# An attention stage and two mixtures of experts on one core: an overflow-only table, a gathered weight table, token counts and the order of loads and fillers are rearranged

## The chip, the cores and the metric

The kernel runs on one core of one Trainium2 chip. The metric is the device time of one execution in microseconds (us). The kernel before was timed three times: 796.45 us is the median, 795.43 the lowest and 799.09 the highest. The trace is of a separate profiled execution.

The names of the engines: PE is the matrix engine, PEld its weight loads, DVE the vector engine, ACT the scalar engine, POOL the GpSimd engine, and SP the engine that here only issues DMA transfers.

## The reference

```python
# 1. attention with decay: x (4,8,768,32), a (4,8,768), B and C (4,8,768,16), in chunks of 32
la = log_a[:, :, sl]; cum = np.cumsum(la, axis=-1)
M = np.einsum('bhin,bhjn->bhij', Cc, Bc) * exp(cum_i - cum_j) * causal
y[:, :, sl] = M @ xc + (Cc @ state) * exp(cum)[..., None]
state = exp(sum(la)) * state + sum_j Bc_j xc_j exp(cum_last - cum_j)
x = y.transpose(0, 2, 1, 3).reshape(3072, 256)
# 2. first mixture: 8 experts (256 -> 1024 -> 256), each token goes to one
probs = softmax(x @ w_gate); expert_idx = argmax(x @ w_gate)
for e in range(8):
    out[mask] = gate_w[mask, None] * (np.maximum(x[mask] @ w1[e], 0) @ w2[e])
# 3. second mixture: 4 experts of the same sizes, each sees all 3072 tokens
p = domain_probs / (domain_probs.sum(-1, keepdims=True) + 1e-9)
out = sum(p[:, e:e + 1] * (np.maximum(x @ w1[e], 0) @ w2[e]) for e in range(4))
```

All arrays are fp32.

## The kernel before

**Attention, to about 102 us.** The 3072 tokens are 24 tiles (`NU`) of 128. A loop `i = 0..24` is written as a software pipeline: in iteration `i` the scores of tile `i+1`, the matmuls `y` of tile `i` (`within`, `across`, L507), and the transposing matmuls and the store of tile `i-1` (`stage_c`, `store`) are issued. There is no scheduler here: each engine runs its instructions in the order in which the program writes them, so an instruction that waits holds back everything behind it on its engine. `load` fetches two tiles of `xb`; `load_bc` fetches a block `cz` (128 x 3 x 384 floats, 576 KB) into one of three buffers, and `bc_head` scales it on ACT to `cm`. `store` copies the router's logits `lg` and the tile `xo` out of PSUM on ACT and sends `xo` to the array `xs` in DRAM. On SP eight DMA semaphores are used in turn, so that a transfer is issued only when the one eight places before it has landed.

**The opening** loads `au`, clips it to `ah`, and makes decay factors by the matmuls `abc` (`decay`, L469) and `pfp` (`decays_c`, L451). `warm(n)` puts `n` matmuls of a unit matrix in front of them, whose result nothing uses.

**Expert 0's weights** come in the loop as well. `WEIGHTS` and `SPLITS` say in which iteration a half of `w1` or `w2` begins to be loaded, and in which its split into a high and a low part begins. A half comes in four pieces, one per iteration (L142); the split takes four steps of two functions each, the high part a cast on ACT (L159), the low part a subtraction on POOL. The pieces of `w1` are column blocks and each cast needs the piece that it reads. The pieces of `w2` are row groups, while each cast takes a column block of all four: the first cast needs all pieces.

```python
WEIGHTS = {1: (0, 0), 5: (0, 1), 9: (1, 0), 13: (1, 1)}
SPLITS = {5: (0, 0), 9: (0, 1), 13: (1, 0), 17: (1, 1)}
...
    for f in ws[:2]:
        f()
    ws = ws[2:]
```

**Routing** follows in three groups of tiles, as they are finished (`GROUPS`). `route` gives a list of small functions (one-hot of the largest logit, `ranks` of the tokens within an expert by matmuls into `rk`, places, and `invert`, which turns the places into lists of tokens by one-hot products `om` and matmuls `ip`). They stand in `queue` and are taken by `slot()` at set points of an iteration; a `None` ends what one call takes. `early()` uses the count of expert 0 after the second group, and `ct` (L1016 to L1020) counts the tokens of all experts when all are routed.

**First mixture, about 102 to 268 us.** For each expert `gemm1x` (L273) makes the hidden values, with products of high and low parts, ACT the relu `hh`, DVE the remainder `hl` (L893), and `gemm2x` the output. Hooks after each step call `prep`, which splits the next expert's weights, and empty the lists `rest` and `queue`. In the queue stand also `places`, `weights2`, the last `invert` with `placed`, and 24 `fetch`es, that gather the weights of the second mixture by token from the DRAM table `pgd`. The list of places in DRAM, `idd`, has its tail filled with zeros in the attention loop (L741) and its body written by `placed` (L1062). Only the block `If left > 0` behind the first mixture reads it, for tokens that found no place; this execution does not take it.

**Second mixture, to the end.** The first weights of it, the pairs of blocks `v`, are loaded by `load_pair` (L177) and prepared by `sums_pair` (L187), whose sums overwrite part of the loaded tile, and `split_pair` (L193 to L197), in the hooks of expert 7. In the mixtures the order on an engine is settled when the kernel is built and is not everywhere the written one.

Of the kernel before, what the change touches and what calls it, by code (L numbers as in the profile page):

```python
# [43 lines left out]
def body(tc, I, out):  # L44
    nc = tc.nc
    with ExitStack() as outer:
# [25 lines left out]
        idc = cp.tile([P, NU], I32, name="idc")  # L72
        pgs = cp.tile([P, NU, E2], F32, name="pgs")
# [127 lines left out]
        def prep(g, step):  # L201
            if g == E1:
                if step < 2 and (g, step) not in RAW:
                    load_pair(g, step)
# [5 lines left out]
            elif g < E1:  # L210
                k = (g, step // 2, step % 2)
                if k not in RAW:
                    load_w(*k)
                fs = split_w(*k, 1 + k[1])
                m = 2 if k[1] else len(fs)
                for f in fs[:m]:
                    f()
                rest.extend(fs[m:])

        def invert(rt, place, g0, n, ncol, finish, psum, bufs=2, off=0, eng=nc.vector):  # L220
# [25 lines left out]
            def mm():  # L246
                ip = o["ip"] = psum([P, ncol], name="ip")
                for i in range(n):
# [5 lines left out]
                    + hots + [None, None, mm, None] + [lambda: finish(o["ip"])])  # L254
# [57 lines left out]
        with ExitStack() as ctx:  # L312
# [32 lines left out]
            bc_part, bc_head = load_bc(0)  # L345
            bc_part(0, P, nc.scalar)
# [3 lines left out]
            nc.scalar.copy(d0, zero.bitcast(F32))  # L350

# [225 lines left out]
            def route(g0, n, psum, between=()):  # L577
# [24 lines left out]
                def ranks():  # L602
                    rk = o["rk"] = psum([P, n, E1], name="rk")
                    nc.tensor.matmul(rk, tri_b, oh, start=True, stop=False)
                    for i in range(n - 1):
                        nc.tensor.matmul(rk[:, i + 1:, :], ones_b,
                                         oh[:, i:i + 1, :].broadcast_to([P, n - 1 - i, E1]), start=False, stop=False)
                    nc.tensor.matmul(rk, ones_b, before[:, None, :].broadcast_to([P, n, E1]),
                                     start=False, stop=True)

                def finish(ip):
# [15 lines left out]
                    lambda: (v.tensor_mul(rs, o["rk"], oh), between and between[0]()),  # L627
                    lambda: v.tensor_reduce(r1, rs, axis=AX.X, op=ALU.add),
                    lambda: v.scalar_tensor_tensor(sl, r1, float(TRASH), m2, op0=ALU.min, op1=ALU.subtract),
                ] + list(between[1:]) + invert(rt, sl, g0, n, NC, finish, psum, off=OFF, eng=g if not g0 else v)  # L630
# [19 lines left out]
            def early():  # L650

                o = {}

                def count():
                    o["c"] = psum_a([P, E1], name="c0")
                    nc.tensor.matmul(o["c"], ones_b, before, start=True, stop=True)

                def shift():
                    v = nc.vector
                    c = o["c"][:, 0:1]  # L660
# [7 lines left out]
                return ([count, shift],  # L668
# [27 lines left out]
            warm(9)  # L696
            chunks[1]()
            decay(0)
            warm(2)
# [21 lines left out]
            WEIGHTS = {1: (0, 0), 5: (0, 1), 9: (1, 0), 13: (1, 1)}  # L721
            SPLITS = {5: (0, 0), 9: (0, 1), 13: (1, 0), 17: (1, 1)}
            DECAYS = {max(3 * m - 2, 2): m for m in range(1, NU // 3)}
            CHUNKS = {0: 3, 1: 4, 2: 2, 3: 5}
            for i in range(NU + 1):
# [14 lines left out]
                if i == 8:  # L740
                    nc.sync.dma_start(idd[NT:], zero)  # L741
                    queue += probs
# [179 lines left out]
        with ExitStack() as ctx:  # L922
# [93 lines left out]
            ct = pp.tile([P, E1], F32, tag="oneA", name="ct")  # L1016
            nc.tensor.matmul(ct, ones_b, before, start=True, stop=False)
            for u in range(ENDS[1] + 1, NU):
                nc.tensor.matmul(ct, ones_b, oneh[:, u], start=False, stop=(u == NU - 1))
            nc.scalar.copy(cnt, ct)  # L1020
# [38 lines left out]

            def placed(ip):  # L1060
                v.tensor_scalar(idc, ip, float(NT // 2), None, op0=ALU.add)
                nc.sync.dma_start(idd[:NT].rearrange("(u p) o -> p (u o)", p=P), idc)  # L1062

            def weights2():
                nc.gpsimd.tensor_mul(prob, prob, gate[:, :, None].broadcast_to([P, NU, E2]))
                nc.sync.dma_start(pgd.rearrange("(u p) e -> p u e", p=P), prob)

            def fetch(u):
                with tc.issue_after(LOW[0]) if LOW else ExitStack():
                    nc.gpsimd.indirect_dma_start(  # L1070
                        pgs[:, u, :], None, pgd, bass.IndirectOffsetOnAxis(ap=idc[:, u:u + 1], axis=0))
# [43 lines left out]
            with tc.If(left > 0), tc.tile_pool(name="fall", bufs=1) as fp:  # L1115
# [3 lines left out]

                st, n, ni, pc, lt = t8("st", (E1,)), t8("n", (E1,)), t8("ni", (E1,), I32), t8("pc", (E1,)), t8("lt", (E1, E1))  # L1120
# [286 lines left out]
```

## Time and profile before

| what | value |
|---|---|
| median of three timed runs | 796.45 us |
| the profiled execution's own time | 799.93 us |
| its span (first to last instruction) | 798.1 us |
| mean granted clock of PE, as a share of full speed | 0.98 |
| PE busy | 763.2 us, 96% |
| DVE, POOL, ACT busy | 573.2, 490.9, 414.1 us |
| DMA, mean over the span | 58 GB/s |

The span is what the trace shows; 1.8 us of the execution's time lie around it. Busy times of different engines overlap. A granted clock of 1.0 is 2.4 GHz, of 0.5 is 1.2 GHz; a value between them over a window is a mixture of the two.

### The profile page before, as it was taken

The page shows a single profiled execution, that of the slowest core. Times are in us where ns is not written, and L with a number is a line of the kernel's source. Part 1 is how long each engine was busy: PE and PEld are TensorE (multiplying, and loading weights), DVE is VectorE, ACT ScalarE, POOL GpSimd, SP SyncE. Part 2 cuts the span into 40 slices and gives each one's busy share as a digit, 9 for nine tenths or more (in the row PEclk, how much of TensorE's full clock was granted, in tenths as well). Part 3 has the DMA queues.
Part 4 walks back from the last instruction along what each step waited for, and adds up shares of the span by engine and source line. Part 5 has one row for each costly group of instructions (what it writes and reads, how often), then busy time and mean ns, then how long its engine had stood idle before and what let it go on. Part 6 is the DMA issues. An engine that isn't in the chain of part 4 may idle for free.

```text
span 798.1 us, 16869 instructions
## 1 busy us (share of the span) xinstructions
PE 763.2 (96%) x6508; PEld 714.8 (90%) x6508; DVE 573.2 (72%) x980; ACT 414.1 (52%) x939; POOL 490.9 (62%) x581
## 2 busy tenths in 40 slices
PE   8979889999998999999999999999999999999994
PEld 5555589899998899999999999999999999999894
DVE  5757955764464787869787678896776987878753
ACT  4656435444554554565655545656456565544540
POOL 4555657557864473658875458776366886575534
PEclk7999999999999999999999999999999999999998
DMA  6686236448531210001110000000001000000001
GB/s 179 178 152 191 76 107 210 96 163 100 163 107 54 55 54 1 1 11 44 28 27 2 1 2 27 27 27 28 1 1 28 28 1 1 1 35 21 27 27 53
DMA packets 41522, 46.57 MB, mean 58 GB/s; under 512 B 10592, under 2 KB 31072, under 8 KB 41440
## 3 DMA queue, kind: packets, MB, share of 16 engines
q1 hardware_dynamic: 36624, 37.09, 17.7%
q0 software_dynamic: 3360, 7.13, 2.9%
q10 hardware_dynamic: 1456, 1.25, 0.5%
q8 instruction: 52, 0.85, 0.5%
q14 instruction: 30, 0.25, 0.1%
HBM read 39.10 MB, written 6.35 MB: 57 GB/s over the span
## 4 chain that ended last, share of the span: by engine, by line
PE 59%; ACT 3%; DVE 2%; issue 1%; POOL 0%; POOLq 0%; ACTq 0%; DVEq 0%
PE po L1292 32%; PE x L1226 9%; PE z L1226 8%; PE w L1226 7%; PE y L1226 3%; ACT xc L852 1%; ACT s L1239 1%; DVE xc L853 1%; ACT h L1232 1%; DVE c L1266 0%; DVE c L1254 0%; POOL out L1312 0%; ACT s L1241 0%; DVE h L1235 0%; PE poA L1292 0%
## 5 line engine op out<-in xcount | busy, mean ns | idle before, releaser
L1292 PE MATMUL po<-w,h 128*128 128x256 f32 x2280 | 280.2, 281 | 0.3 <-DVE h L1235 0.3
L1292 PEld LDWEIGHTS po<-w,h 128*128 128x128 f32 x2280 | 277.6, 188 | 0.5 <-DVE h L1235 0.5
L1232 ACT ACTIVATE h<-c 128x384 fp32r<-128x384 f32 x192 | 98.6, 525 | 160.8 <-DVE c L1266 92.1
L1235 DVE SCALAR_TENSOR_TENSOR h<-c,h 128x384 fp32r<-128x384 f32 x192 | 153.3, 807 | 18.1 <-ACT h L1232 6.9
L1245 POOL TENSOR_TENSOR g<-s,s 128x384 f32<-128x384 f32 x64 | 65.0, 1016 | 110.4 <-ACT s L1243 110.4
L165 POOL TENSOR_TENSOR wl<-raw,wh 128x256 fp32r<-128x256 f32 x72 | 54.5, 783 | 54.1 <-ACT wh L159 52.9
L853 POOL TENSOR_TENSOR xc<-ts,xc 128x384 fp32r<-128x384 f32 x61 | 71.1, 1174 | 25.2 <-PE x L1226 14.0
L1247 DVE TENSOR_TENSOR u<-y,s 128x384 f32<-128x384 f32 x64 | 35.4, 553 | 57.4 <-ACT s L1243 57.1
L1226 PE MATMUL x<-xc,wh 128*128 128x384 f32 x256 | 68.4, 348 | 5.0 <-ACT s L1239 4.0
L1226 PE MATMUL w<-xc,wh 128*128 128x384 f32 x256 | 65.7, 337 | 0.5 <-DVE xc L853 0.5
L1226 PE MATMUL z<-xc,wh 128*128 128x384 f32 x256 | 65.5, 337 | 0.0
L1266 DVE TENSOR_TENSOR c<-u,g 128x384 f32<-128x384 f32 x63 | 64.5, 1024 | 0.0
L853 POOL TENSOR_TENSOR xc<-x,xc 128x384 fp32r<-128x384 f32 x31 | 36.4, 1173 | 42.7 <-ACT xc L852 42.7
L891 ACT ACTIVATE hh<-ph 128x216 fp32r<-128x216 f32 (+8 forms) x68 | 32.9, 491 | 49.1 <-PE ph L273 41.0
L273 PE MATMUL ph<-xh,wh 128*128 128x480 f32 (+8 forms) x142 | 49.6, 349 | 4.4 <-DVE hl L893 3.6
L1239 ACT COPY s<-x 128x384 f32<-128x384 f32 x64 | 30.5, 476 | 44.2 <-PE x L1226 44.2
L1235 DVE SCALAR_TENSOR_TENSOR h<-x,h 128x384 fp32r<-128x384 f32 x64 | 35.6, 557 | 24.2 <-ACT h L1232 23.5
L1226 PEld LDWEIGHTS x<-xc,wh 128*128 128x128 f32 x256 | 41.4, 188 | 12.2 <-ACT s L1239 10.2
L893 DVE SCALAR_TENSOR_TENSOR hl<-ph,hh 128x216 fp32r<-128x216 f32 (+8 forms) x68 | 36.7, 551 | 18.4 <-ACT hh L891 18.3
L273 PE MATMUL ph<-xl,wh 128*128 128x480 f32 (+8 forms) x142 | 48.4, 341 | 0.0
L273 PE MATMUL ph<-xh,wl 128*128 128x480 f32 (+8 forms) x142 | 48.2, 339 | 0.0
L912 PE MATMUL po<-hh,wh 128*128 128x480 f32 (+8 forms) x142 | 48.1, 339 | 0.0
(243 smaller groups left out, 1690.9 us busy)
## 6 DMA issues: line engine op xcount, KB each, us to landing
raw<-in_w SPq DMA_DIRECT2D x26, 512.0 KB, 4.1
raw<-in_v SPq DMA_DIRECT2D x32, 256.0 KB, 2.7
xb<-in_xb SPq DMA_DIRECT2D x22, 192.0 KB, 4.4
cz<-in_cb SPq DMA_DIRECT2D x7, 576.0 KB, 7.0
xs<-xo SPq DMA_DIRECT2D x24, 128.0 KB, 3.3
raw<-in_w SPq DMA_DIRECT2D x16, 128.0 KB, 5.1
raw<-in_w ACTq DMA_DIRECT2D x2, 512.0 KB
xg<-xs,idr POOLq DMA_INDIRECT x26, 3.9
```

Source lines behind the costliest of these rows:

```text
L165: ins = nc.gpsimd.tensor_sub(lo[:, :, a:a + n], raw[:, :, a:a + n], hi[:, :, a:a + n].bitcast(F32))
L273: mm = nc.tensor.matmul(ph, w[:, k, fs], x[k], start=(i == 0), stop=(i == 5))
L853: eng.tensor_sub(o[:, 1], src, o[:, 0].bitcast(F32))
L893: i1 = nc.vector.scalar_tensor_tensor(hl, ph, 0.0, hh.bitcast(F32), op0=ALU.max, op1=ALU.subtract)
L912: mm = nc.tensor.matmul(po, w[:, f % 4, ks], h, start=(i == 0), stop=(i == 23))
L1226: nc.tensor.matmul(bank[to], w[:, a], x[:, r], start=(m == 0 and to not in seen), stop=(m == 2), skip_group_check=True)
L1232: sc.activation(HP[n][0], src, AF.Relu)
L1235: v.scalar_tensor_tensor(HP[n][1], src, 0.0, HP[n][0].bitcast(F32), op0=ALU.max, op1=ALU.subtract)
L1239: sc.copy(s1, bank["x"])
L1245: nc.gpsimd.tensor_add(g_, s5, s7)
L1266: v.tensor_add(c22, u2, g_)
L1292: nc.tensor.matmul(two[h], x[:, ts], w2[:, w, j], start=(i, j, h * (len(hs) - 1), m) == (0, 0, 0, 0), stop=(i, j, m) == (3, 1, 2), skip_gr ...
```

## The change

1. The list of places `idd` is no longer written in the loop (L741) and in `placed` (L1062), but inside the block `If left > 0`.
2. The table of weights by token, `pgd`, is written with a partition's 24 rows together (`(p u) e`) instead of a tile's 128 rows together. The index of the gather is then not the token's number but its place in that table; `placed` computes it into `idg` with four more small operations on DVE.
3. The count of tokens per expert becomes one more slot of `rk`: `ranks` starts with the ones-matmul on `before`, adds the one-hots, and ends with the triangular one. `count` in `early` and the six matmuls `ct` with their copy go; `cnt` is copied from `rk`. `invert` has one more `None` ahead of the matmuls `ip`.
4. The first two pairs of blocks of the second mixture are loaded right behind the splits of expert 7's `w2` (through `rest`), and no longer at the head of `prep(E1, step)`.
5. In the opening ACT issues its load of the first third of `cz` behind the copy `d0` instead of ahead of it; `warm` has 10 and 4 matmuls instead of 9 and 2.
6. `WEIGHTS` starts one iteration earlier, `SPLITS` two.

```diff
         def prep(g, step):
             if g == E1:
-                if step < 2 and (g, step) not in RAW:
-                    load_pair(g, step)
                 if step < 3:
...
                 rest.extend(fs[m:])
+                if g == E1 - 1 and k[1]:
+                    rest.append(lambda: load_pair(E1, k[2]))
...
-                    + hots + [None, None, mm, None] + [lambda: finish(o["ip"])])
+                    + hots + [None, None, None, mm, None] + [lambda: finish(o["ip"])])
...
-            bc_part, bc_head = load_bc(0)
-            bc_part(0, P, nc.scalar)
             d0 = ac.tile([P, 1], F32, name="d0")
             ah = ac.tile([P, H, L], F32R, name="ah")
             nc.gpsimd.memset(ah[:, :, 0:1].bitcast(F32), 0.0)
             nc.scalar.copy(d0, zero.bitcast(F32))
+            bc_part, bc_head = load_bc(0)
+            bc_part(0, P, nc.scalar)
...
-                    rk = o["rk"] = psum([P, n, E1], name="rk")
-                    nc.tensor.matmul(rk, tri_b, oh, start=True, stop=False)
-                    for i in range(n - 1):
+                    rk = o["rk"] = psum([P, n + 1, E1], name="rk")
+                    nc.tensor.matmul(rk, ones_b, before[:, None, :].broadcast_to([P, n + 1, E1]),
+                                     start=True, stop=False)
+                    for i in range(n):
                         nc.tensor.matmul(rk[:, i + 1:, :], ones_b,
-                                         oh[:, i:i + 1, :].broadcast_to([P, n - 1 - i, E1]), start=False, stop=False)
-                    nc.tensor.matmul(rk, ones_b, before[:, None, :].broadcast_to([P, n, E1]),
-                                     start=False, stop=True)
+                                         oh[:, i:i + 1, :].broadcast_to([P, n - i, E1]), start=False, stop=False)
+                    nc.tensor.matmul(rk[:, :n], tri_b, oh, start=False, stop=True)
...
-                    lambda: (v.tensor_mul(rs, o["rk"], oh), between and between[0]()),
+                    lambda: (v.tensor_mul(rs, o["rk"][:, :n], oh), last and nc.scalar.copy(cnt, o["rk"][:, n])),
...
-            warm(9)
+            warm(10)
             chunks[1]()
             decay(0)
-            warm(2)
+            warm(4)
             decays_c(0)
...
-            WEIGHTS = {1: (0, 0), 5: (0, 1), 9: (1, 0), 13: (1, 1)}
-            SPLITS = {5: (0, 0), 9: (0, 1), 13: (1, 0), 17: (1, 1)}
+            WEIGHTS = {0: (0, 0), 4: (0, 1), 8: (1, 0), 12: (1, 1)}
+            SPLITS = {3: (0, 0), 7: (0, 1), 11: (1, 0), 15: (1, 1)}
...
                 if i == 8:
-                    nc.sync.dma_start(idd[NT:], zero)
                     queue += probs
...
-            ct = pp.tile([P, E1], F32, tag="oneA", name="ct")
-            nc.tensor.matmul(ct, ones_b, before, start=True, stop=False)
-            for u in range(ENDS[1] + 1, NU):
-                nc.tensor.matmul(ct, ones_b, oneh[:, u], start=False, stop=(u == NU - 1))
-            nc.scalar.copy(cnt, ct)
...
             def placed(ip):
                 v.tensor_scalar(idc, ip, float(NT // 2), None, op0=ALU.add)
-                nc.sync.dma_start(idd[:NT].rearrange("(u p) o -> p (u o)", p=P), idc)
+                v.tensor_scalar(t24, ip, float(NT // 2), float(NU), op0=ALU.add, op1=ALU.mult)
+                v.tensor_scalar(tile0, ip, float(NT // 2) - 63.5, float(BIG), op0=ALU.add, op1=ALU.add)
+                v.tensor_scalar(tile0, tile0, -float(BIG), 1.0 / P - NU, op0=ALU.add, op1=ALU.mult)
+                v.tensor_add(idg, t24, tile0)
...
-                nc.sync.dma_start(pgd.rearrange("(u p) e -> p u e", p=P), prob)
+                nc.sync.dma_start(pgd.rearrange("(p u) e -> p u e", p=P), prob)
...
+                nc.sync.dma_start(idd[:NT].rearrange("(u p) o -> p (u o)", p=P), idc)
+                nc.sync.dma_start(idd[NT:], zero)
```

**SP, iterations 8 to 12 of the attention loop, before** (`raw0` is a piece of `w1`, `raw1_0_0` and `raw1_0_1` are pieces of the two halves of `w2`, `xs` is the store of a tile):

```order
L741 DMA idd_68<-zero_70 128x1
L575 DMA xs_66<-xo_870 256x1x128
L142 DMA raw1_0_0_913<-in_w2 128x256
L575 DMA xs_66<-xo_938 256x1x128
L436 DMA xb1_147<-in_xb 64x2x384 x2
L142 DMA raw1_0_0_913<-in_w2 128x256
L575 DMA xs_66<-xo_1012 256x1x128
L337 DMA cz0_130<-in_cb 128x1152
L142 DMA raw1_0_0_913<-in_w2 128x256
L575 DMA xs_66<-xo_1078 256x1x128
L436 DMA xb2_148<-in_xb 64x2x384 x2
L142 DMA raw1_0_0_913<-in_w2 128x256
```

and in the changed kernel, from the same place:

```order
L143 DMA raw1_0_0_852<-in_w2 128x256
L576 DMA xs_66<-xo_881 256x1x128
L143 DMA raw1_0_0_852<-in_w2 128x256
L576 DMA xs_66<-xo_946 256x1x128
L437 DMA xb1_148<-in_xb 64x2x384 x2
L143 DMA raw1_0_0_852<-in_w2 128x256
L576 DMA xs_66<-xo_1020 256x1x128
L338 DMA cz0_131<-in_cb 128x1152
L143 DMA raw1_0_0_852<-in_w2 128x256
L576 DMA xs_66<-xo_1088 256x1x128
L437 DMA xb2_149<-in_xb 64x2x384 x2
L143 DMA raw1_0_1_1133<-in_w2 128x256
```

The write of `idd` is gone, and each piece of `w2` stands one iteration earlier; directly behind `cz0` stands now the fourth piece of `raw1_0_0` and not the third.

**ACT, before, around the first cast of `w2`** (on SP the fourth piece stands ahead of the store of `xo_1147`; `xo_1216` is the next tile's; `wh1` is the high part):

```order
L454 COPY pfg1_150<-pfp_1209 128x96x2
L455 COPY pf_1211<-pfp_1209 128x384
L573 COPY lg_99<-tp_1202 128x8
L574 COPY xo_1216<-tp_1202 128x264
L525 COPY yT_1245<-y_1220 128x2x2x64
L159 CAST wh1_0_0_1188<-raw1_0_0_913 128x4x64
```

and in the changed kernel, where `xo_1088` is what the store behind the fourth piece sends:

```order
L574 COPY lg_100<-tp_1078 128x8
L575 COPY xo_1088<-tp_1078 128x264
L526 COPY yT_1117<-y_1092 128x2x2x64
L341 ACTIVATE cm_850<-cz2_133,hmask_160 128x384 x2
L160 CAST wh1_0_0_1064<-raw1_0_0_852 128x4x64
L532 COPY U_1145<-S_1135 128x32
```

The first cast of `w2` stood in the iteration after that in which its last piece is issued, and stands now in the same iteration; `U`, the state's copy, which the next tile needs, stands right behind it on ACT.

**DVE, before, the begin of expert 7** (`raw0_8_0` and `raw0_8_2` are the tiles of `v` of the first and the third pair, on which `sums_pair` makes four sums each, `wl1_7` the low part of expert 7's `w2`, `hl` its hidden remainder):

```order
L307 TENSOR_TENSOR xl_3816<-tpx_3817,xh_3815 128x2x256
L307 TENSOR_TENSOR xl_3816<-tpx_3824,xh_3815 128x2x128
L187 TENSOR_TENSOR raw0_8_2_3967<-raw0_8_2_3967 128x128
L163 TENSOR_TENSOR wl1_7_0_3858<-raw1_7_0_3855,wh1_7_0_3857 128x4x128
L187 TENSOR_TENSOR raw0_8_2_3967<-raw0_8_2_3967 128x128 x3
L917 ISA
L917 COPY x21_2077<-po_3861 128x380
L163 TENSOR_TENSOR wl1_7_1_3890<-raw1_7_1_3887,wh1_7_1_3889 128x4x128
L893 SCALAR_TENSOR_TENSOR hl_3894<-ph_3909,hh_3893 128x368
```

and in the changed kernel:

```order
L308 TENSOR_TENSOR xl_3818<-tpx_3826,xh_3817 128x2x128
L164 TENSOR_TENSOR wl1_7_0_3860<-raw1_7_0_3857,wh1_7_0_3859 128x4x128
L911 ISA
L911 COPY x21_2082<-po_3863 128x380
L164 TENSOR_TENSOR wl1_7_1_3892<-raw1_7_1_3889,wh1_7_1_3891 128x4x128
L887 SCALAR_TENSOR_TENSOR hl_3896<-ph_3911,hh_3895 128x368
L164 TENSOR_TENSOR wl1_7_0_3860<-raw1_7_0_3857,wh1_7_0_3859 128x4x128
L164 TENSOR_TENSOR wl1_7_1_3892<-raw1_7_1_3889,wh1_7_1_3891 128x4x128
L887 SCALAR_TENSOR_TENSOR hl_3898<-ph_3933,hh_3897 128x368
L887 SCALAR_TENSOR_TENSOR hl_3900<-ph_3943,hh_3899 128x368
L887 SCALAR_TENSOR_TENSOR hl_3902<-ph_3953,hh_3901 128x368
L188 TENSOR_TENSOR raw0_8_0_3922<-raw0_8_0_3922 128x128 x3
```

The third pair's sums stood ahead of the splits and of all of expert 7's remainders. In the changed kernel the first sums on this engine are those of the first pair, behind four of the remainders; the third pair's stand behind the first two's.

## Rows read from the trace of the kernel before

**Rows 1.** The page's first part: busy time, share and instructions of each engine.

```profile
PE 763.2 (96%) x6508; PEld 714.8 (90%) x6508; DVE 573.2 (72%) x980; ACT 414.1 (52%) x939; POOL 490.9 (62%) x581
```

**Rows 2.** Windows: start:end, length, busy us (instructions) PE PEld DVE ACT POOL, clock, DMA share, GB/s.

```profile
8.50:22.00 13.50, 13.32 (x167) 6.78 (x169) 7.65 (x11) 5.65 (x19) 6.86 (x19) 0.50 0.55 155
50.00:55.00 5.00, 2.96 (x81) 1.79 (x68) 0.80 (x1) 1.88 (x7) 2.85 (x6) 1.00 0.99 59
55.00:60.00 5.00, 2.99 (x68) 1.97 (x68) 2.42 (x4) 1.86 (x7) 0.00 (x0) 0.63 0.70 149
60.00:65.00 5.00, 5.00 (x82) 2.94 (x74) 2.96 (x4) 3.12 (x11) 1.78 (x3) 0.69 0.88 279
185.00:190.00 5.00, 5.00 (x27) 4.83 (x27) 1.64 (x3) 1.08 (x3) 4.07 (x5) 1.00 0.95 34
250.00:255.00 5.00, 2.06 (x9) 1.76 (x10) 5.00 (x13) 0.95 (x2) 0.24 (x1) 0.93 0.14 30
255.00:260.00 5.00, 5.00 (x24) 5.00 (x23) 3.06 (x9) 2.67 (x5) 0.00 (x0) 0.73 0.27 93
```

**Rows 3.** Timeline, opening: start us, us, engine line operation out<-in, [idle before <-releaser].

```profile
5.19 0.29 DVE L417 TENSOR_SCALAR ah<-au 128x252 fp32r<-128x252 f32 x1 [1.06 <-DMA au<-in_au]
...
6.41 0.47 PE L469 MATMUL abc<-ah,pk 128*128 128x512 f32 x1 [0.96 <-ACT cm L340]
6.71 0.61 PE L426 MATMUL warm<-ident 128*128 128x128 f32 x4
8.19 1.32 PE L451 MATMUL pfp<-spare,sel 32*128 32x384 f32 x2 [0.87 <-DVE spare L397]
```

**Rows 4.** Timeline of PE, line 507 alone: some of the tiles' matmuls `y`.

```profile
15.48 0.68 PE L507 MATMUL y<-M,xb 64*32 64x64 f32 x32
20.20 0.68 PE L507 MATMUL y<-M,xb 64*32 64x64 f32 x32
25.71 0.46 PE L507 MATMUL y<-M,xb 64*32 64x64 f32 x32
28.53 0.45 PE L507 MATMUL y<-M,xb 64*32 64x64 f32 x32
...
52.66 0.30 PE L507 MATMUL y<-M,xb 64*32 64x64 f32 x4
57.01 0.76 PE L507 MATMUL y<-M,xb 64*32 64x64 f32 x28 [4.05 <-issue]
62.04 0.68 PE L507 MATMUL y<-M,xb 64*32 64x64 f32 x32
```

**Rows 5.** Timeline of SP around the write of `idd`: the write, and the ninth transfer from it.

```profile
45.43 0.42 SPq L741 DMA_DIRECT2D idd<-zero  x1
...
55.92 2.15 SPq L337 DMA_DIRECT2D cz<-in_cb  x1
```

**Rows 6.** Tile `idd`, the second write (L1062, at 179.1): from issue to landing.

```profile
DMA to landing us min/median/max: 15.1/15.1/15.1
```

**Rows 7.** Tile `raw` on SP, the piece issued at 34.8 (behind a `cz`).

```profile
L142 SPq DMA_DIRECT2D raw<-in_w x1: 443/443/443, 34.8 to 34.8; - x1
...
DMA to landing us min/median/max: 6.8/6.8/6.8
```

**Rows 8.** The same view, the piece issued at 27.9.

```profile
DMA to landing us min/median/max: 2.5/2.5/2.5
```

**Rows 9.** The page's sixth part, all pieces: count, KB each, median us to landing.

```profile
raw<-in_w SPq DMA_DIRECT2D x16, 128.0 KB, 5.1
```

**Rows 10.** Timeline of ACT, the cast in the iteration of the piece of rows 7.

```profile
36.93 0.39 ACT L159 CAST wh<-raw 128x256 fp32r<-128x256 f32 x1
```

**Rows 11.** Waits of DVE from 239 to 262: total us, times, longest.

```profile
DVE raw L187 <- DMA raw<-in_v: 7.7, 1, 7.7
```

**Rows 12.** Timeline, expert 7's begin: SP's loads of `v`, and PE's first stop.

```profile
239.25 7.76 SPq L177 DMA_DIRECT2D raw<-in_v  x2
...
252.55 0.43 PE L273 MATMUL ph<-xh,wh 128*128 128x368 f32 x1 [2.56 <-DVE hl L893]
```

**Rows 13.** Timeline of PE, the counts before.

```profile
107.06 0.27 PE L1019 MATMUL ct<-oneh,ones_b 128*128 128x8 bf16 x5
```

More of the change, by code (lines that the diff above doesn't have):

```diff
@@ L72, in body @@
         idc = cp.tile([P, NU], I32, name="idc")
+        idg = cp.tile([P, NU], I32, name="idg")
         pgs = cp.tile([P, NU, E2], F32, name="pgs")
@@ L626, in route @@
                     None,
-                    lambda: (v.tensor_mul(rs, o["rk"], oh), between and between[0]()),
+                    lambda: (v.tensor_mul(rs, o["rk"][:, :n], oh), last and nc.scalar.copy(cnt, o["rk"][:, n])),
                     lambda: v.tensor_reduce(r1, rs, axis=AX.X, op=ALU.add),
                     lambda: v.scalar_tensor_tensor(sl, r1, float(TRASH), m2, op0=ALU.min, op1=ALU.subtract),
-                ] + list(between[1:]) + invert(rt, sl, g0, n, NC, finish, psum, off=OFF, eng=g if not g0 else v)
+                    lambda: [f(o["rk"][:, n, 0:1]) for f in between],
+                ] + invert(rt, sl, g0, n, NC, finish, psum, off=OFF, eng=g if not g0 else v)
             load(0, 1)
@@ L650, in early, with shift @@
             def early():
[L652 to L658, printed above, removed]
+                def shift(c):
                     v = nc.vector
-                    c = o["c"][:, 0:1]
                     v.tensor_scalar(enough, c, float(CAP0 - GAP0), None, op0=ALU.is_ge)
@@ L667, in early @@
                 ie = m1.tile([P, 2], I32, name="ie")
-                return ([count, shift],
+                return ([shift],
                         [lambda: nc.vector.tensor_scalar(ie, idxf[:, 0:2], float((EARLY + 1) * P - 1), None, op0=ALU.min)]
@@ L1058, in places @@
                 v.tensor_add(place, place, rank)
+            t24 = rt("t24", [P, NU], F32, 1)
+            tile0 = rt("tile0", [P, NU], F32, 1)
             def placed(ip):
                 v.tensor_scalar(idc, ip, float(NT // 2), None, op0=ALU.add)
-                nc.sync.dma_start(idd[:NT].rearrange("(u p) o -> p (u o)", p=P), idc)
+                v.tensor_scalar(t24, ip, float(NT // 2), float(NU), op0=ALU.add, op1=ALU.mult)
+                v.tensor_scalar(tile0, ip, float(NT // 2) - 63.5, float(BIG), op0=ALU.add, op1=ALU.add)
+                v.tensor_scalar(tile0, tile0, -float(BIG), 1.0 / P - NU, op0=ALU.add, op1=ALU.mult)
+                v.tensor_add(idg, t24, tile0)
             def weights2():
                 nc.gpsimd.tensor_mul(prob, prob, gate[:, :, None].broadcast_to([P, NU, E2]))
-                nc.sync.dma_start(pgd.rearrange("(u p) e -> p u e", p=P), prob)
+                nc.sync.dma_start(pgd.rearrange("(p u) e -> p u e", p=P), prob)
             def fetch(u):
@@ L1070, in fetch @@
                     nc.gpsimd.indirect_dma_start(
-                        pgs[:, u, :], None, pgd, bass.IndirectOffsetOnAxis(ap=idc[:, u:u + 1], axis=0))
+                        pgs[:, u, :], None, pgd, bass.IndirectOffsetOnAxis(ap=idg[:, u:u + 1], axis=0))
             queue = turn_steps + [places, gates, gates2, weights2] + [f for f in invert(
```

## The prediction

> **What bounds the kernel.** I read the busy times first. PE is busy 96% of the span and DVE, the next, 72% [rows 1], so only what starts, stops or slows PE counts. Next I read PE's clock and busy time by windows [rows 2] and PE's own timeline, looking for idle time and for stretches at half clock. Apart from the very end they lie at three places that the change touches.
>
> The opening: PE stops 0.96 us before `abc` and 0.87 us before `pfp` [rows 3]. Then its granted clock is 0.50, the lower of its two levels (1.2 GHz), from 8.5 to 22 us, and it is busy 13.32 of those 13.50 us [rows 2]. From one tile's `y` to the next it takes 4.72 us there (15.48 to 20.20) and 2.82 us later at full clock (25.71 to 28.53) [rows 4].
>
> The attention loop at 53 us: the matmuls `y` of one tile stop 4.05 us after the first four of 32, for nothing that the profile shows as a releaser, and the clock is at its lower level for part of the next ten microseconds [rows 2, 4].
>
> The begin of expert 7: DVE waits 7.7 us for a tile of `v` [rows 11]. Behind this wait on DVE stand `hl` and the splits of `w2`, and PE stops 2.56 us for `hl` [rows 12]. The clock falls again, to means of 0.93 and 0.73 in the next two windows of 5 us [rows 2].
>
> **The cost of each part.** All terms are against the profiled execution's own time, 799.93 us, which is 3.5 us above the median.
>
> *List of places.* The write of zeros is issued at 45.43, and `cz`, the eighth transfer behind it, which needs the same semaphore, at 55.92 [rows 5]. So the write took up to 10.5 us. In between the DMA engines are 99% busy and move 59 GB/s; in 60 to 65 they move 279 at 88% [rows 2]. Busy at so low a rate is what I would see if many tiny writes held the engines. The second write of the list is of the same form: it lands after 15.1 us [rows 6], with 95% busy at 34 GB/s in 185 to 190, but there PE is busy 5.00 of 5.00 us and loses nothing [rows 2]. The same jam costs only where PE needs something from DRAM; for the stop at 53 I take that to be its instructions, since nothing else is shown as awaited.
> From `y` at 52.66 to the next tile's at 62.04 it took 9.38 us, against about 2.9 for a tile [rows 4]. The loss is **-6.5**. It is at least the stop, 4.0, and at most the stop and the time at half clock: means of 0.63 and 0.69 over 5 us each are 3.7 and 3.1 us at the lower level [rows 2], half of which is lost, so 7.5. The second write, and the new layout of `pgd`, lie under a PE without gaps, and so do the four DVE operations behind them: 0. If that cover were gone, the write's 15.1 us would delay the gathers behind it, which is a gain here.
>
> *Load of the first pairs of `v`.* The wait of DVE was on a load whose issue SP held from 239.25 for 7.76 us [rows 12]. In the changed order `hl` and the splits of expert 7 no longer stand behind sums on `v`; four `hl` go first. This removes the stop of 2.56 [rows 12], and the time at half clock: 0.7 us in the first window and 2.7 in the second [rows 2], of which half, 1.7, is lost. Sum **-4.3**, and at least -2.5 if another wait brings the clock down. Late next are the sums of the first pair, which stand behind four `hl` and have the rest of expert 7 to get done.
>
> *Opening.* `abc` waits for `ah`, for which DVE waited 1.06 us on the load of `au` [rows 3]. ACT's load of `cz` shared the DMA engines with it; issued behind the copy it is out of the way, and I take 0.7 us of the 1.06 as saved. Three more fillers, at 0.15 us each (four in 0.61) [rows 3], fill 0.45 us more of the 1.83 us that PE stood, so that some 0.7 remains. I take this as enough to keep the clock at its higher level, though no row shows the limit. What that is worth: at full clock 13.32 us of PE work shrink to about 0.6 (2.82 to 4.72) of it, so by up to 5.3. DVE has only 7.65 us of work in the window [rows 2] and doesn't stop this, but waits between engines don't shrink with the clock; I take 3.3. Together **-4.0**, between -0.5 (earlier `abc` alone, clock as before) and -5.5.
>
> *Weights of expert 0.* The split is moved two iterations forward, the loads only one. For `w1` a cast needs one piece and had four iterations of slack, now three: 0. For `w2` the first cast needs all four pieces, and the last is now issued in the same iteration, for the first half right behind a `cz`. A piece in that position, issued at 34.8, landed 6.8 us later [rows 7]; the median of all is 5.1 [rows 9], and the fastest I looked up took 2.5 [rows 8]. The cast of such an iteration runs 2.1 us behind the piece's issue (36.93 against 34.8) [rows 7, 10]. So ACT would wait 0.4 to 4.7 us, with the copy `U` behind it, which the next tile's matmuls need, and POOL's subtractions behind the cast. I take 3.7 for the first half, of which PE has some slack, so 3.3, and 1.0 for the second, which has no `cz` ahead of it: **+4.3**, between 0 and +9 (4.7 twice, less a little).
>
> *Counts.* The matmuls that go take 0.3 us (five in 0.27) [rows 13]; a slot of 8 columns more per ranking matmul and one later `None` before `ip` cost about as little: **-0.5**, with the copy gone from the wait of `turns`; bounds -1 and +1.
>
> The sum is -4.0 - 6.5 + 4.3 - 4.3 - 0.5 = **-11.0 us**: 788.9 for the profiled execution, and against the median 796.45 - 11.0 = **785.5**. A measurement of this kernel can tell about 0.5% (4 us) from no change.
>
> **The rivals.**
>
> *The fillers do not hold the clock* (0.22). For it: the trace shows only that stops of 0.96 and 0.87 were followed by the lower level, and I leave some 0.7. Then of the opening only 0.7 remains: 785.5 + 3.3 = 788.8.
>
> *The pieces of `w2` land in time* (0.15). For it: one landed in 2.5 us [rows 8], and without the jam, in which most of `w2`'s first half was loaded, the queue is emptier. Against it: the slow one of rows 7 was not in the jam. Then 785.5 - 4.3 = 781.2. The Trainium skill, "DMA: Bandwidth & Descriptors", section "Anatomy of one DMA — SWDGE (gpsimd) path", gives 2.0 us and bytes over 436 GB/s for a transfer that GpSimd issues. By that a piece of 128 KB would take an estimated 2.3 us, and this rival would be the rule; the trace agrees at one piece and disagrees at the median.
>
> *The stop at 53 is not the list's* (0.07). Its releaser is not shown, and PE's stop would then come again at another time: only the other terms hold, 785.5 + 6.5 = 792.0. The same page of the Trainium skill, section "Queues, rings and completion order", says that each DMA engine changes between the queues it has work for after every packet, so that tiny writes on SP's queue should not hold up another queue's transfer for microseconds. By that rule the term of 6.5 would be nothing; the 99% at 59 GB/s speaks against it, and no row names what PE waited for.
>
> *The sums still hold `hl` up* (0.04), because the load is not in fact earlier or the wait is taken by a split: 785.5 + 4.3 = 789.8.
>
> *Slower* (0.04). The price of the early `w2` splits is larger than all gains: ACT waits 6.8 us at each half [rows 7] and PE stops so long that its clock falls each time, which after the stop at 53 cost 3.4 us: 2 x (6.8 + 3.4) = 20.4 in place of 4.3, so 785.5 + 16.1 = 801.6. It decides from about 15 us lost at these two casts. Against it: PE is fed by DVE and the matmuls ahead of `U` in the meantime, and the piece is on its way for 2 us before ACT comes.
>
> **How the numbers follow.** My forecast gets the remaining 0.48: 785.5. Range: the first two rivals and the bounds of the jam (+2.5, -1.0) and of the opening (-1.5) give 779 to 791; the third rival reaches 792. I give **779 to 792**, leaving out the slower case and the tails of two errors in one direction. Faster by over 0.5% is below 792.5: nearly all of the forecast, the first, second and fourth rivals and half of the third, 0.87. Within 0.5%: 0.09. Slower: 0.04.
>
> **What would show it.** Right: between 45 and 60 us no window with DMA share near 0.99 at under 100 GB/s, `cz` issued without the stand of SP, and `y` every 3 us or so; PE's clock 1.0 between 8.5 and 22; no wait of DVE at L188 near 245, and a clock of 1.0 from 250 to 260; a new wait of ACT for a piece of `w2` at the casts in iterations 11 and 15, some 3 us at the first. Wrong: a stop of PE for nothing shown while `idd` is no longer written; a lower clock in the opening all the same; a wait at the casts over 6 us, or a result above 792.

## The result and the profile after

| | median | runs | ratio to the kernel before |
|---|---|---|---|
| before, same chip | 798.03 us | 795.43 to 800.88 | 1 |
| changed | 790.72 us | 789.63 to 795.11 | 0.9914, 95% interval 0.9888 to 0.994 |

The change saves 0.86%, 6.9 us by the ratio. The forecast was 785.5, 11 us less than the median shown then. The profiled execution after took 790.72 us with a span of 788.9, 9.2 less than that of before: this pair of profiles shows more than the medians do. Single runs over 1.5% above the fastest of the same kernel are left out of all medians and ranges below.

The page's first part, after: PE's share is as in [rows 1], with 3.2 us less of busy time.

```profile
PE 760.0 (96%) x6510; PEld 713.3 (90%) x6510; DVE 572.4 (73%) x984; ACT 414.6 (53%) x939; POOL 492.9 (62%) x581
```

Windows of the changed kernel (columns as in [rows 2]), with one from 22 to 30 us:

```profile
8.50:22.00 13.50, 11.41 (x234) 6.44 (x236) 9.79 (x14) 8.56 (x27) 8.07 (x21) 0.96 0.89 246
22.00:30.00 8.00, 8.00 (x191) 4.79 (x183) 4.63 (x7) 6.27 (x22) 5.15 (x9) 0.85 0.45 122
50.00:55.00 5.00, 2.94 (x85) 1.69 (x73) 2.98 (x4) 2.05 (x6) 0.58 (x2) 1.00 0.89 262
55.00:60.00 5.00, 4.03 (x43) 2.33 (x51) 1.62 (x3) 2.34 (x9) 3.39 (x6) 0.51 0.26 69
60.00:65.00 5.00, 5.00 (x145) 3.24 (x146) 3.31 (x7) 3.05 (x12) 1.86 (x3) 0.80 0.45 117
250.00:255.00 5.00, 5.00 (x32) 5.00 (x31) 4.46 (x12) 2.58 (x5) 0.00 (x0) 1.00 0.33 116
255.00:260.00 5.00, 4.67 (x27) 4.14 (x26) 1.89 (x4) 0.79 (x3) 0.00 (x0) 1.00 0.33 102
```

In the opening the clock is 0.96 and not 0.50, and PE is left idle for two of the 13.5 us: it waits 1.1 us for ACT's `cm` and 0.9 for its `rhsT`. From 22 to 30 the clock still falls once, to a mean of 0.85. From 50 to 55 the engines of DMA move 262 GB/s at 89%, and not 59 at 99%: the jam is gone. Yet PE is busy only 2.94 of these 5.00 us, as before, and the clock falls again. At 250 nothing stops.

The opening of PE and the stop at 53, after (timeline of PE, then of ACT, POOL and SP):

```profile
6.17 0.77 PE L470 MATMUL abc<-ah,pk 128*128 128x512 f32 x1
6.74 1.35 PE L427 MATMUL warm<-ident 128*128 128x128 f32 x8
8.10 0.88 PE L452 MATMUL pfp<-spare,sel 32*128 32x384 f32 x2
...
49.31 0.46 PE L508 MATMUL y<-M,xb 64*32 64x64 f32 x32
52.12 0.46 PE L508 MATMUL y<-M,xb 64*32 64x64 f32 x32
55.97 0.66 PE L541 MATMUL U<-xb,br 128*32 128x64 f32 x16 [3.03 <-POOL br L481]
59.86 0.68 PE L508 MATMUL y<-M,xb 64*32 64x64 f32 x32
...
54.34 0.40 ACT L160 CAST wh<-raw 128x256 fp32r<-128x256 f32 x1 [2.53 <-DMA raw<-in_w]
70.34 0.40 ACT L160 CAST wh<-raw 128x256 fp32r<-128x256 f32 x1 [0.98 <-DMA raw<-in_w]
...
54.82 0.72 POOL L166 TENSOR_TENSOR wl<-raw,wh 128x256 fp32r<-128x256 f32 x1 [4.42 <-ACT wh L160]
55.50 0.41 POOL L481 TENSOR_TENSOR br<-xb,Lt 128x128 f32<-128x128 f32 x1
...
49.12 0.33 SPq L338 DMA_DIRECT2D cz<-in_cb  x1
49.52 0.42 SPq L143 DMA_DIRECT2D raw<-in_w  x1
```

Read from the bottom: SP issues `cz` and right behind it the last piece of the first half of `w2`. The cast on ACT waits until 54.34 for it, 4.8 us behind its issue. POOL's low part waits for the cast, `br` stands behind the low part on POOL, and PE's `U` waits for `br`: a stop of 3.03 us, and then the lower clock. The wait that the prediction added is there, link by link. The second cast row is the first of the second half.

The start of a tile's `y` gives the ledger, since PE does the same work between two of them in all profiles (us from the span's start; the last five rows are kernels of the experiments):

```
tile               0      3     11     12     13     14     23
before         15.48  28.53  52.66  62.04  65.41  68.23  99.25
after          12.51  25.18  49.31  52.12  59.86  63.53  94.71
after_again    12.29  23.52  47.63  50.44  61.57  66.46 100.02
late_w2_again  12.52  23.75  47.87  50.68  53.64  57.22  88.06
late_zero      12.55  23.79  48.21  54.28  57.80  61.77  93.97
open_back      14.55  26.95  51.08  53.90  63.83  66.64  97.36
late_fill      13.66  24.88  49.01  51.82  54.79  57.98  88.77
```

Before against after: -3.35 us until tile 11 (opening), -6.57 from 11 to 12 (9.38 to 2.81, jam), +5.22 from 12 to 14 (6.19 to 11.41, wait for `w2`), +0.16 to tile 23, -4.52 from there to the first matmul of the second mixture (268.37 and 259.31), and -0.14 behind it. The sum is -9.2, the difference of the spans. This after is one execution: the other ten profiles with 10 and 4 fillers have tile 3 at 23.25 to 24.20, so it shows less of the opening than they do.

### The profile page after: what moved, and what is told of

Read it like the earlier page. It is cut to its first block, busy times and chain, and to the rows that moved or that the text cites. A ratio compares the mean times of both kernels' runs of the same rounds, so it can differ in the third digit from the quotient of the medians.

```text
span 788.9 us, 16870 instructions
## 1 busy us (share of the span) xinstructions
PE 760.0 (96%) x6510; PEld 713.3 (90%) x6510; DVE 572.4 (73%) x984; ACT 414.6 (53%) x939; POOL 492.9 (62%) x581
## 4 chain that ended last, share of the span: by engine, by line
PE 59%; ACT 3%; issue 2%; DVE 1%; POOL 1%; POOLq 0%; ACTq 0%; DVEq 0%
PE po L1289 32%; PE x L1223 9%; PE z L1223 8%; PE w L1223 7%; PE y L1223 3%; ACT xc L846 1%; POOL out L1309 1%; ACT s L1236 1%; DVE c L1263 1%; ACT h L1229 1%; DVE xc L847 0%; ACT s L1238 0%; DVE c L1251 0%; ACT s L1240 0%; PE poA L1289 0%
## 5 line engine op out<-in xcount | busy, mean ns | idle before, releaser
L1263 DVE TENSOR_TENSOR c<-u,g 128x384 f32<-128x384 f32 x63 | 66.6, 1057 | 0.0
L887 DVE SCALAR_TENSOR_TENSOR hl<-ph,hh 128x216 fp32r<-128x216 f32 (+8 forms) x68 | 36.9, 551 | 16.6 <-ACT hh L885 15.1
L906 PE MATMUL po<-hl,wh 128*128 128x480 f32 (+8 forms) x142 | 47.7, 336 | 1.0 <-POOL hl L266 1.0
```

The lines of the kernel that those rows point to most:

```text
L887: i1 = nc.vector.scalar_tensor_tensor(hl, ph, 0.0, hh.bitcast(F32), op0=ALU.max, op1=ALU.subtract)
L906: mm = nc.tensor.matmul(po, w[:, f % 4, ks], h, start=(i == 0), stop=(i == 23))
L1263: v.tensor_add(c22, u2, g_)
```

## The experiments

The experiments ran in three groups of four kernels, each group on another chip with runs of the kernel before beside it (medians 796.32, 796.89 and 798.01 us). Each result is a median in us, with its ratio to the kernel before and the 95% interval of that ratio. Differences are of medians; where the two kernels ran on different chips, the difference between chips is in them.

### The wait for w2

**late_w2** and, in one group with the changed kernel, **late_w2_again**:

```diff
-            SPLITS = {3: (0, 0), 7: (0, 1), 11: (1, 0), 15: (1, 1)}
+            SPLITS = {3: (0, 0), 7: (0, 1), 13: (1, 0), 17: (1, 1)}
```

> The changed kernel with the two splits of w2 begun in iterations 13 and 17 again (as in the kernel before), its loads one iteration earlier as changed. Theory: ACT's cast waited 2.53 us for the last piece of w2 and with it PE stopped 3.03 us and lost half of 6.8 us at half clock; with two iterations more the piece is there, the wait of ACT for raw is gone, the tile that took 7.74 us takes 2.8 to 3.4, and the time falls by 4 to 5 us below the changed kernel, to about 786. Rival: the piece only exposes another late transfer (cz or xb in the same stretch), and PE stops for that one: 789 to 791.

> The changed kernel with the splits of w2 from iterations 13 and 17, again, on the same chip as the changed kernel. Theory (the wait for w2 costs 4 to 6 us): 4 to 6 us under the changed kernel. Rival (what the first comparison showed was the chip's spread): within 1.5 us of it.

**after_again** is the changed kernel itself.

> The changed kernel, measured again beside the three below. It is expected between 789 and 793 us, 0.9 to 1.0% under the kernel before. In its profile ACT waits 2 to 6 us for a piece of w2 at the first cast behind the second cz, since three profiles of kernels with the same loop showed PE stops of 3.0 to 5.5 us there.

Measured: 790.99 for the changed kernel (ratio 0.9916, 0.9883 to 0.9948) and 785.35 for late splits (0.9879, 0.9831 to 0.9927; in the first group 786.65, 0.9855, 0.9812 to 0.9897). So the wait costs 5.6 us by the two medians of one chip, 4.1 to 4.3 by late_w2, and the version with late splits is faster than both kernels. In its profile the stretch from 50 to 60 reads (windows):

```profile
45.00:50.00 5.00, 5.00 (x151) 3.19 (x151) 3.71 (x6) 3.70 (x14) 3.66 (x8) 1.00 0.76 175
50.00:55.00 5.00, 4.66 (x117) 2.88 (x116) 4.03 (x5) 3.67 (x13) 1.63 (x3) 1.00 0.92 291
55.00:60.00 5.00, 4.98 (x113) 3.16 (x114) 3.93 (x11) 3.34 (x10) 1.81 (x3) 1.00 0.64 174
```

PE is hardly idle and the clock is full; from tile 12 to 14 it takes 6.54 us, and no other late transfer stops PE there, as the rival would have it. Without a write in small pieces in the loop, the seven profiles with late splits take 6.2 to 6.8 us there and the four with early ones 11.4 to 16.0. In the second profile of the changed kernel the same chain is longer (timeline of ACT and PE):

```profile
56.04 0.40 ACT L160 CAST wh<-raw 128x256 fp32r<-128x256 f32 x1 [5.92 <-DMA raw<-in_w]
...
57.68 0.66 PE L541 MATMUL U<-xb,br 128*32 128x64 f32 x16 [6.42 <-POOL br L481]
```

With 6.42 us of stop it takes 16.02 us from tile 12 to 14. Two executions of one program thus differ by 4.6 us at this place, and by 5.2 in all (spans of 788.9 and 794.1). The rest does not stand still either: the second is 1.7 us shorter up to tile 11 and 2.4 longer from tile 14 to 23, where its clock is 0.50 from 85 to 90 us. So the wait can account for much of the changed kernel's spread, 787 to 796; that it does is not shown.

### The list of places

**zero_back**, in the changed kernel, and **late_zero**, the same edit beside late splits:

```diff
                 if i == 8:
+                    nc.sync.dma_start(idd[NT:], zero)
                     queue += probs
...
-                nc.sync.dma_start(idd[NT:], zero)
```

> The changed kernel with the write of zeros to the list of places put back into iteration 8 of the attention loop. Theory: the DMA engines are about 99% busy at under 100 GB/s for 5 to 10 us behind it, PE stops for 4 us or more and loses clock, and the time rises by 5 to 7 us over the changed kernel, less what overlaps with the wait for w2. Rival: the jam is not from this write, and the time stays within 1 us of the changed kernel.

> The same kernel with late splits of w2, and the write of zeros to the list put back into iteration 8. No split waits for w2 here, so it shows the jam by itself. Theory (the write's jam costs the 6.5 us of the prediction, by its instructions that PE waits for): PE stops some 4 us between 47 and 58 us, for nothing that the profile shows, DMA near 99% at under 100 GB/s; 6 to 7 us more than with late splits alone. Rival (the jam only delays transfers that have slack): 0 to 2 us more.

**late_zero_row**, as late_zero with the zeros on one partition:

```diff
+            zrow = ac.tile([1, P], I32, name="zrow")
+            nc.gpsimd.memset(zrow, 0)
...
                 if i == 8:
+                    nc.sync.dma_start(idd[NT:].rearrange("(a p) o -> a (p o)", a=1), zrow)
                     queue += probs
...
-                nc.sync.dma_start(idd[NT:], zero)
```

> As late_zero, but the same 512 bytes of zeros go out from one partition as one row instead of four bytes from each of 128 partitions. Theory (the number of tiny pieces makes the jam, not the write): no window at 99% with under 100 GB/s, no stop of PE there, within 1 us of the late splits alone. Rival (any transfer at this place of the queue jams): the same 6 us as late_zero.

Measured: zero_back 794.56 (0.9978, 0.9952 to 1.0005), 3.6 to 3.8 over the changed kernel's two medians and 0.62 to 0.64% over its two ratios, 5 us; its theory said 5 to 7. late_zero 790.36 (0.9919, 0.9885 to 0.9952), 5.0 over late splits alone, where 6 to 7 were expected. late_zero_row 786.55 (0.9872, 0.983 to 0.9913), 1.2 over them, not told apart from 0. The same 512 bytes as one row cost nothing to be seen; as 128 pieces of four bytes they cost about 5 us. First late_zero, with SP's rows, SP's wait for the write, a window and the two stops, then late_zero_row:

```profile
40.67 0.38 SPq L736 DMA_DIRECT2D idd<-zero  x1
50.59 0.33 SPq L338 DMA_DIRECT2D cz<-in_cb  x1
...
SPq L338 <- DMA idd<-zero: 3.4, 1, 3.4
...
45.00:50.00 5.00, 4.52 (x140) 2.88 (x140) 3.21 (x4) 2.54 (x10) 3.34 (x7) 1.00 0.77 77
...
50.89 0.38 ACT L575 COPY xo<-tp 128x264 f32<-128x264 f32 x1 [2.64 <-DMA xs<-xo]
...
51.75 0.27 PE L541 MATMUL U<-xb,br 128*32 128x64 f32 x2 [2.14 <-issue]
```

```profile
40.49 0.33 SPq L738 DMA_DIRECT2D idd<-zrow  x1
47.60 0.34 SPq L338 DMA_DIRECT2D cz<-in_cb  x1
...
45.00:50.00 5.00, 5.00 (x152) 3.24 (x152) 3.71 (x6) 3.80 (x14) 3.64 (x8) 1.00 0.73 190
```

With small pieces `cz` is issued 9.9 us behind the write, and SP waits 3.4 us of them for the write to land. With the row it is 7.1, and SP does not wait for the row (47.60, against 47.76 in late_w2_again with no write at all). About the same DMA share, 77 and 73%, moves 77 GB/s and not 190. The prediction took the stop for a wait on instructions. The profile of before fits that: the DMA view from 50 to 55 us shows the packets of queue 8, which carries instructions (packets, MB, share of 16 engines):

```profile
q8 instruction: 1, 0.02, 8.3%
```

8.3% of 16 x 5 us is 6.6 us for one packet. The same row of late_w2_again, without the write, says:

```profile
q8 instruction: 1, 0.02, 1.5%
```

That is 1.2 us. The slow packet begins at 51.0, so it ends at 57.7, while PE stands from 53.0 to 57.01: the two overlap, and that PE waited for this packet is not shown. In late_zero no instruction packet is slow: there ACT waits 2.64 us until an earlier store has freed its buffer, and PE stops 2.14 for nothing shown, behind 14 of 16 matmuls `U`. zero_back stops at the same place, 1.91 us. So the jam is the small pieces', but what PE waits for in it stays open.

**late_tables**, beside late splits, puts the other write of the list, and the old layout of `pgd`, back into the first mixture; the four operations for `idg` go, and the gathers take `idc` again:

```diff
             def placed(ip):
                 v.tensor_scalar(idc, ip, float(NT // 2), None, op0=ALU.add)
+                nc.sync.dma_start(idd[:NT].rearrange("(u p) o -> p (u o)", p=P), idc)
...
-                nc.sync.dma_start(pgd.rearrange("(p u) e -> p u e", p=P), prob)
+                nc.sync.dma_start(pgd.rearrange("(u p) e -> p u e", p=P), prob)
```

> Late splits of w2, and in the first mixture the list of places written from all 3072 tokens to DRAM again and the table of weights by token written and gathered in the old layout. Theory: the DMA engines are above 90% at under 50 GB/s for 5 to 15 us around 170 to 190, PE stays busy 5.00 of 5.00 us there, and the time is within 1 us of the base. Rival: the fetches by GpSimd come late and push the second mixture or its preparation: 2 us or more over the base.

Measured: 790.12 (0.9877, 0.9833 to 0.9922), six runs from 785 to 792. Windows and PE's stop:

```profile
175.00:180.00 5.00, 5.00 (x32) 4.86 (x31) 2.53 (x5) 3.48 (x6) 4.25 (x7) 1.00 0.75 19
180.00:185.00 5.00, 5.00 (x28) 4.84 (x27) 0.81 (x2) 0.00 (x0) 4.07 (x5) 1.00 0.93 43
190.00:195.00 5.00, 4.17 (x21) 3.49 (x20) 3.42 (x7) 4.15 (x8) 1.68 (x2) 1.00 0.92 275
...
191.53 0.46 PE L273 MATMUL ph<-xh,wh 128*128 128x408 f32 x1 [0.50 <-DVE hl L886]
193.24 0.46 PE L273 MATMUL ph<-xh,wh 128*128 128x408 f32 x1 [0.33 <-DVE hl L886]
```

The jam is back, 93% at 43 GB/s, and behind it PE stops for 0.83 us in all, which it did not in the profile of before; both stops are for DVE's `hl`, and that the jam made `hl` late is not shown. The median is 3.3 to 4.7 over the two kernels of its group that are near the base (below), so the theory's 1 us did not come and the rival's 2 us or more did, but the intervals overlap. Its profile doesn't give these microseconds to the tables: tile 23 starts at 91.90, 3.8 us later than in late_w2_again, and the clock is 0.60 and 0.71 from 95 to 105 (0.72 and 1.00 there), all ahead of the edit's first transfer at 144.5. So at most 0.8 us is seen where the edit acts, and what the rest is stays open.

### The opening

**open_back** undoes both edits of the opening; **late_fill**, beside late splits, undoes only the two `warm` lines of this diff, and **late_cz** only the place of the load:

```diff
+            bc_part, bc_head = load_bc(0)
+            bc_part(0, P, nc.scalar)
             d0 = ac.tile([P, 1], F32, name="d0")
...
             nc.scalar.copy(d0, zero.bitcast(F32))
-            bc_part, bc_head = load_bc(0)
-            bc_part(0, P, nc.scalar)
...
-            warm(10)
+            warm(9)
...
-            warm(4)
+            warm(2)
```

> The changed kernel with the opening as before: ACT's load of cz ahead of its first copy, 9 and 2 fillers. Theory: PE stops again about 0.9 us twice before 8.2 us, the clock is at its lower level from 8.5 to 22, and the tiles from 3 on are 3.3 us later: the time rises by 3 to 3.4 us. Rival: the lower clock between 21 and 24 us, which the changed kernel still has, only moves, and the time rises by 1 us or less.

> Late splits of w2 (the base of these four, 785.4 and 786.7 us in two measurements), and the fillers of the opening as before: 9 and 2. Theory of the prediction (it is the fillers that hold the clock): the clock is at its lower level from about 9 us for 10 us or more, the first y stands 2 us later, and the time rises by 2.5 to 3.5 us. Rival (the earlier load of au does it): PE stops a little longer but the clock holds; within 1 us of the base.

> Late splits of w2, and ACT's load of the first third of cz ahead of its first copy as before, with the 10 and 4 fillers kept. Theory: abc is 0.3 to 0.7 us later, since the load of au shares the DMA engines with cz, but the fillers hold the clock: 0.3 to 1 us over the base. Rival: PE stops long enough that the clock falls, 3 us over the base.

Measured: open_back 791.02 (0.9927, 0.9899 to 0.9955), which can't be told from the changed kernel: not its theory's 3 to 3.4 us came but its rival's number, 1 us or less. late_fill 789.94 (0.9894, 0.9863 to 0.9926), 3.1 over late_cz, 786.86 (0.9848, 0.9808 to 0.9888), whose own distance from the base, 785.35 and 786.65, can't be told from 0. The intervals of late_fill and late_cz overlap; six of late_fill's eleven runs lie above the highest of late_cz. late_fill spreads from 785.4 to 794.7, late_cz from 784.9 to 789.0; open_back, from 786.9 to 794.6, spreads no more than the changed kernel does. The stops are the same in both kernels with few fillers, 0.48 us ahead of `abc` and 0.87 ahead of `pfp`, shown here for open_back, and the clock from 8.5 to 22 is lower in both, but not equally. The windows are of open_back, late_fill and late_cz, in this order:

```profile
6.15 0.47 PE L470 MATMUL abc<-ah,pk 128*128 128x512 f32 x1 [0.48 <-DVE ah L420]
7.93 0.88 PE L452 MATMUL pfp<-spare,sel 32*128 32x384 f32 x2 [0.87 <-DVE spare L398]
...
8.50:22.00 13.50, 12.17 (x178) 6.52 (x181) 8.07 (x12) 7.20 (x23) 7.53 (x19) 0.62 0.67 171
```

```profile
8.50:22.00 13.50, 11.47 (x189) 6.29 (x188) 9.12 (x14) 7.63 (x23) 7.99 (x20) 0.87 0.82 209
```

```profile
8.50:22.00 13.50, 11.42 (x257) 6.70 (x260) 9.38 (x14) 8.99 (x29) 8.51 (x21) 1.00 0.92 246
```

A mean of 0.62 is 10.3 us at the lower level of the clock, 0.87 is 3.5, and [rows 2] had all of 13.5. Tile 3 starts at 26.95, 24.88 and, in late_cz, 23.31. In all eleven profiles with 10 and 4 fillers the mean of this window is 0.96 or more, in the three with 9 and 2 it is 0.50, 0.62 and 0.87. So the fillers keep the clock up here, and the place of the load does nothing that shows. What they give in time is less sure: about 3 us beside late splits, nothing to be told beside early ones; why the two differ stays open.

### The first pairs of v, and the counts

**pair_back**, in the changed kernel:

```diff
             if g == E1:
+                if step < 2 and (g, step) not in RAW:
+                    load_pair(g, step)
...
-                if g == E1 - 1 and k[1]:
-                    rest.append(lambda: load_pair(E1, k[2]))
```

> The changed kernel with the load of the first two pairs of v at the head of the second mixture's preparation again. Theory: DVE waits 7 to 8 us for raw, PE stops about 2.6 us and loses another 1.7 by the clock: the time rises by 4.3 to 4.7 us. Rival: the change of the order of DVE's sums came from the splits of expert 0 or from the counts, DVE's wait stays away, and the time stays within 1 us.

Measured: 794.84 (0.9966, 0.9936 to 0.9996), 3.9 to 4.1 over the changed kernel. DVE's wait and the window of PE's stop are back. The load that DVE waits for comes first here, from SP, with who waited for it:

```profile
L178 SPq DMA_DIRECT2D raw<-in_v x1: 352/352/352, 242.5 to 242.5; - x1
  DVE raw L188: 7.6, 1
...
DVE raw L188 <- DMA raw<-in_v: 7.6, 1, 7.6
...
245.00:250.00 5.00, 2.42 (x10) 2.13 (x9) 4.72 (x12) 1.17 (x3) 0.94 (x1) 0.80 0.03 5
250.00:255.00 5.00, 5.00 (x27) 5.00 (x27) 3.86 (x10) 3.15 (x6) 0.00 (x0) 0.86 0.33 103
```

The changed kernel's load at this place, and DVE's longest wait for a load of `v` from 235 to 257 us in it:

```profile
L178 SPq DMA_DIRECT2D raw<-in_v x1: 352/352/352, 243.2 to 243.2; - x1
...
DVE raw L188 <- DMA raw<-in_v: 0.5, 1, 0.5
```

So in time the load has not moved forward, 242.5 against 243.2; what the edit changed is what DVE does first, `hl` and the splits ahead of the sums.

**late_counts**, beside late splits:

```diff
-                    rk = o["rk"] = psum([P, n + 1, E1], name="rk")
+                    rk = o["rk"] = psum([P, n, E1], name="rk")
...
+            ct = pp.tile([P, E1], F32, tag="oneA", name="ct")
+            nc.tensor.matmul(ct, ones_b, before, start=True, stop=False)
...
-                    + hots + [None, None, None, mm, None] + [lambda: finish(o["ip"])])
+                    + hots + [None, None, mm, None] + [lambda: finish(o["ip"])])
```

> Late splits of w2, and the counts by their own matmuls (c0 and ct) again, with ip one slot earlier. Theory: within 1 us of the base, with 0.3 us of matmuls ct behind the attention loop; the gap of PE in the first expert is 0.4 and not 1.0 us. Rival: the ip one slot earlier makes PE wait for the one-hots of DVE, 1 to 2 us over the base.

Measured: 785.40 (0.9834, 0.9795 to 0.9874), as the base: the counts give nothing that a measurement tells. The gap of PE in the first expert, 0.98 us in the changed kernel's profile, is 0.44 in late_w2, which has the counts as changed, so the longer gap is not theirs.

## Why the prediction was right, and where it was too large

The time lies in the range, in its upper part, and on the forecast side, and the four large terms all show in the trace. The saving is 6.9 us and not 11, and it is a matter of sizes, and of what they were taken from:

| term | forecast | this pair of profiles | medians of the experiments |
|---|---|---|---|
| opening | -4.0 | -3.35 | -3.1 (late_fill) to 0 (open_back) |
| list of places in the loop | -6.5 | -6.57 | -5.0 (late_zero), -3.6 to -3.8 (zero_back) |
| early splits of `w2` | +4.3 | +5.2, +9.8 in the second profile | +5.6 (late_w2_again), +4.1 to +4.3 (late_w2) |
| first pairs of `v` | -4.3 | -4.5 with all behind tile 23 | -3.9 to -4.1 |
| counts | -0.5 | in the line above | 0 |
| tables in the first mixture | 0 | none | not told from 0; 0.8 of stops in one profile |

- **The base of the sum.** The terms were counted in one execution of 799.93 us and taken off a median of 796.45. From 799.93 they give 788.9, and the profiled execution after took 790.72, 1.8 more. The median of before on this chip turned out at 798.03, so the execution that was read was 1.9 us dear, and what made it dear can be among the terms. That 790.72 lies in the range owes something to the range's width: 785.5 was missed by 5.2.
- **Early splits of w2** were mis-sized most. The step said that ACT would wait 3.7 us for the first half, "of which PE has some slack, so 3.3", and 1.0 for the second. The waits were 2.53 and 5.92, the stops of PE 3.03 and 6.42, so PE had no slack, and the half clock behind the stop, which that term left out, came on top: means of 0.51 and 0.80 from 55 to 65 are 6.9 us at the lower level, of which half is lost. At the second half ACT waited 0.98 us in the first profile, as forecast, and not at all in the second; from tile 14 to 23 the first took 31.18 us against 31.02 before, so next to nothing of it reached PE. That the landing is slow was right: the piece had landed 4.8 us behind its issue, where 3.7 of wait behind 2.1 meant 5.8. The fit of the Trainium skill, "DMA: Bandwidth & Descriptors", section "Anatomy of one DMA — SWDGE (gpsimd) path", is for transfers that GpSimd issues; by it the piece, which SP issues, would take an estimated 2.3 us, and the trace disagrees with 4.8.
- **The jam** was 6.5 in the trace because that trace had it so; by medians of late_zero it is 5.0. A price taken from a single profiled execution was the high end. That the many small pieces make the jam is shown by the one-row version; that PE waited for its instructions is not.
- **The opening** was right in kind, and its first half, 0.7 us for an earlier `abc`, was 0.24 (6.41 to 6.17), and not even that is the load's: with the old order of the load `abc` starts at 6.15 in open_back and at 5.90 in late_cz. In late_fill and open_back it is not the stops that vary but how long the lower clock lasts.
- **The first pairs of v** were right to some tenths, stop and clock together. A reading beside them was not: the row of 7.76 us [rows 12] is two issues merged, the second at 246.7 and 0.35 us long, and not one that SP held. DVE waited for this second one, which landed 2.6 us behind its issue.
- **The rivals.** The fillers held the clock; the pieces did not land in time; the stop was the list's. The load of `v` was indeed not earlier, but the sums no longer held `hl` up. The same page of the Trainium skill, section "Queues, rings and completion order", says that a DMA engine changes between its queues after every packet. What the prediction drew from it, that tiny writes should not hold up another queue's transfer for microseconds, is at odds with the 6.6 us that one instruction packet took before, against 1.2 without the write.

## What to carry to other kernels

A term that a change adds must be given its clock too: here waits of 2.5 and 5.9 us on an engine that feeds PE were paid as PE's stop and as the slower stretch behind it. Before a consumer is moved forward, see that its last load moves by as much, or leave the consumer: the late splits with early loads beat both kernels, 785.35 against 796.89 and 790.99 on one chip. No run here moved the loads further. And take a price from several executions where there are some; a single trace can be the dear one.

## What was not expected of the hardware

- A transfer of 512 bytes in pieces of four put off the next use of its semaphore to 9.9 us behind it (10.5 before) and the transfers around it at 77 GB/s; as one row it cost nothing that shows, at 7.1 us and 190 GB/s.
- The same two stops of PE, 0.48 and 0.87 us, were followed by 3.5 us at the lower clock in the profile of late_fill and 10.3 in that of open_back.
- Before, the second write of the list landed after 15.1 us [rows 6] and the slowest gather of `pgd` after 15.2 (median 2.7), while PE was busy 5.00 of every 5.00 us from 180 to 195: there a jam of the same kind cost PE nothing.
